# Where a spectral layer asks for its tables and weights: two loads moved from GpSimd's queue to SyncE's, the others asked for earlier, and one table loaded in halves

## The chip, the cores and the metric

The kernel runs on one core of a Trainium2 chip. Its engines are TensorE (PE; its weight loads are listed as PEld), VectorE (DVE), ScalarE (ACT), GpSimd (POOL) and SyncE (SP), each with an instruction stream of its own. They wait for one another by semaphores. Transfers between memory (HBM) and the on-chip memory are asked for by an instruction on SP, ACT or POOL and carried by 16 DMA engines that all queues share; each asking engine has its own queue. The metric is the device time of one execution in microseconds (us), as the median of several runs. A profile is one further execution, recorded instruction by instruction.

## The reference

Two kinds of layer alternate, twice: a spectral layer A and an attention layer B, each on the layer-normed input and added to it.

```python
def _A_ref(x, w_r, w_i):                       # x: [1, 2048, 512]
    X = jnp.fft.rfft2(x.astype(jnp.float32), axes=(-2, -1))
    X = X * (w_r + 1j * w_i)                   # w: [2048, 257]
    return jnp.fft.irfft2(X, s=(S, D), axes=(-2, -1)).astype(jnp.bfloat16)

def _B_ref(x, wq, wk, wv, wo):                 # 32 heads of 16, one shared key and value head
    q = (x @ wq).reshape(B, S, 32, 16).transpose(0, 2, 1, 3)
    k, v = x @ wk, x @ wv
    p = _softmax(jnp.einsum("bhqd,bkd->bhqk", q, k) * 16 ** -0.5, axis=-1)
    o = jnp.einsum("bhqk,bkd->bhqd", p, v)
    return o.transpose(0, 2, 1, 3).reshape(B, S, 512) @ wo

x = A_x
x = x + _A_ref(_layernorm(x), A_w_r, A_w_i)
x = x + _B_ref(_layernorm(x), B_wq, B_wk, B_wv, B_wo)
x = x + _A_ref(_layernorm(x), A_w_r, A_w_i)
x = x + _B_ref(_layernorm(x), B_wq, B_wk, B_wv, B_wo)
```

## The kernel before

The input lies as 16 tiles of 128 rows (`x_sb`, 2 MB in all), in four blocks of four tiles. `full_kernel` asks for the first loads on SP: block 0 of x in two parts, the table `PH` (0.5 MB, the transform along the 512 columns), then blocks 1, 2 and 3 of x with the halves of the tables `S1` and `C1` between them. `feed` takes the layer norm's statistics on DVE, two tiles a step, and makes `S1N`, the negative of `S1`, in two halves.

**The spectral layer** writes the Fourier transforms as matrix products. Its stages, by the names that the profile shows:

- *First loop* (`k` from 0, columns' half `h` = 0): at each step it calls `load(k)` and `feed(k)`, turns two tiles of x (`transpose_pair`, L198 and L201), multiplies them by one half of `PH` (`forward`, L262, result `Pk` on ACT, L184), and rotates them by `C1`, `S1`, `S1N` (`first`, L212 to L214, result `A1`, L274 or L276). Each `A1` goes to memory by a store to `D1` on SP (L277, 128 KB). When the stores that it needs have landed, `cross1` (L280, 256 KB) reads a quarter of `D1` back into `A2` with another part of the rows on the partitions.
- *Second loop* (`h` = 1): `load(10 + k)`, `forward` and `first` with the other half of `PH`, and its own stores and four `cross1`. At k = 7 DVE makes `H2N` from `H2`.
- *Filter loop* (`j` from 0): `filtered(j)` rotates `A2` by the table `G` (L212 to L214, result `X`, L326), and multiplies by the weights `wr_sb` and `wi_sb` on DVE (L330, L332, result `Z`). Steps 0 to 3 read `A2` of the first loop, steps 4 to 7 that of the second. Two steps behind, `back(j)` rotates `Z` by `H1`, `H2N`, `H2` and sends the result `B1` to memory (`D2`, L355).
- Two further stages (`along`, L379, from `B2`, which is read back from `D2`; then `last`) give the columns back and add x.

In the second spectral layer x is turned by DMA transposes during the attention layer before it, save its last tiles, and the last rows of that attention layer's output are made inside the first loop (`rest`).

**What sets the order.** PE, ACT, DVE and SP run in the order in which the code writes their instructions in a spectral layer (`manual_schedule`); POOL isn't in that list, and a scheduler places its instructions. An instruction on SP that waits holds back everything behind it on SP. Eight semaphores go round among the transfers asked for on SP and ACT, so that one also waits for the landing of the one eight before it.

**Where memory is shared.** `wr_sb` lies in the same place as `Kv`, the attention layer's keys (tag `wrkv`). `wi_sb`, `H1` and `H2` lie in a pool of the spectral layer (`tabA`) whose memory the attention layer uses for its own tiles in between. In the second layer their loads wait for the last readers of what lay there. `load` is the function that asks for weights and tables; the weights' runs in memory are 512 bytes long (256 of 257 columns), those of the tables 4096.

Of the kernel before, what the change touches and what calls it, by code (L numbers as in the profile page):

```python
# [11 lines left out]
P = 128  # L12
BF = mybir.dt.bfloat16
# [125 lines left out]
def tile_of(x, k):  # L139
    return x[:, k // 4, k % 4, :]  # L140
# [76 lines left out]
def spectral_layer(nc, tc, tabs, ht, A_w_r, A_w_i, x_sb, bigp, pre, norm, att, feed, weights):  # L217
    C1, S1, S1N, PH, ident = (tabs[n] for n in ("C1", "S1", "S1N", "PH", "ident"))
    with tc.tile_pool(name="workA", bufs=2) as work, tc.tile_pool(name="tabA", bufs=1) as tabA, \
# [7 lines left out]
        wi_sb = tabA.tile([P, 16, 256], BF, name="wi_sb")  # L227
        H1, H2, H2N = (tabA.tile([P, 16, P], BF, name=f"tab_{n}") for n in ("H1", "H2", "H2N"))

        def tables(names):  # L230
            for name in names:
                if tabs[name] is None:
                    tabs[name] = ht.load(tabs["pool"], name)

        def load(k):

            if k == 3:
                nc.sync.dma_start(out=wr_sb, in_=A_w_r.rearrange("(p a) f -> p a f", p=P)[:, :, 1:NF])
            elif k == 6:
                nc.sync.dma_start(out=wi_sb, in_=A_w_i.rearrange("(p a) f -> p a f", p=P)[:, :, 1:NF])  # L240
            elif k == 9:
                tables(("G",))
            elif k == 4:
                ht.load(tabA, "H2", H2, eng=nc.gpsimd)
            elif k == 5:
                ht.load(tabA, "H1", H1, eng=nc.gpsimd)
            elif k == 19:
                tables(("CS", "PSC", "PSS", "hmask"))
            weights(k)
# [35 lines left out]
        for k in range(9 + behind):  # L285
            load(k)
            feed(k, psum)
            if not turned and k < 8:
                transpose_pair(nc, tabs["ident"], psum, x_sb, xT, k, feed.busy or k % 2 == 1, "pa")
            elif turned and LATE_AT <= k < LATE_AT + 2:  # L290
                transpose_pair(nc, tabs["ident"], psum, x_sb, xT, k + 6 - LATE_AT, feed.busy or k % 2 == 1, "pa")
            at = k - behind
            if 0 <= at < 8:
                forward(at, 0)
            if at >= 1:
                first(at - 1, 0)
            if at >= 4 and at % 2 == 0:
                cross1((at - 4) // 2, 0)
        cross1(3, 0)
        for k in range(9):  # L300
            load(10 + k)
            if k < 8:
                forward(k, 1)
            if k >= 1:
                first(k - 1, 1)
            if k >= 4 and k % 2 == 0:
                cross1((k - 4) // 2, 1)
            if k == NEGATE:
                nc.vector.tensor_single_scalar(out=H2N, in_=H2, scalar=-1.0, op=ALU.mult)
        cross1(3, 1)  # L310
        load(19)
        G, CS, PSC, PSS = (tabs[n] for n in ("G", "CS", "PSC", "PSS"))

# [847 lines left out]
@with_exitstack  # L1161
def full_kernel(ctx, tc, A_x, A_w_r, A_w_i, B_x, B_wq, B_wk, B_wv, B_wo, out):
    nc = tc.nc
    const = ctx.enter_context(tc.tile_pool(name="const", bufs=1))
    x_v = A_x.flatten_outer_dims().rearrange("(p r t) d -> p r t d", r=R, t=T)
    x_sb = const.tile([P, R, T, 512], BF, name="x_sb")
    ht = Tables(nc)
    tabs = dict(pool=const, CS=None, PSC=None, PSS=None, hmask=None, G=None)
    tabs["ident"] = ht.load(const, "ident", eng=nc.scalar)
    for part in (slice(0, 2), slice(2, 4)):  # L1170
        nc.sync.dma_start(out=x_sb[:, 0, part, :], in_=x_v[:, 0, part, :])
    tabs["PH"] = ht.load(const, "PH")
    tabs["S1"] = tabs["C1"] = None
    for r in range(1, R):
        nc.sync.dma_start(out=x_sb[:, r, :, :], in_=x_v[:, r, :, :])
        if r < 3:
            for n in ("S1", "C1"):
                tabs[n] = ht.load(const, n, tabs[n], slice(8 * r - 8, 8 * r))
    mhalf = const.tile([P, 4], F32, name="mhalf")
    nc.gpsimd.memset(mhalf, -0.5)  # L1180
    tabs["S1N"] = const.tile([P, 16, P], BF, name="tab_S1N")
    wq_sb = const.tile([P, NC, D], BF, name="wq_sb")
    wk_sb = const.tile([P, NC, DH], BF, name="wk_sb")
    wka = const.tile([P, NC, 8, DH], BF, name="wka")
    wo_sb = const.tile([P, 4, D], BF, name="wo_sb")
    wv_sb = const.tile([P, NC, DH], BF, name="wv_sb")
    xn_sb = const.tile([P, R, T, 512], BF, name="xn_sb")
    lnpool = ctx.enter_context(tc.tile_pool(name="lnpool", bufs=1))
    bigp = ctx.enter_context(tc.tile_pool(name="bigp", bufs=6))
    out_v = out.flatten_outer_dims().rearrange("(p r t) d -> p r t d", r=R, t=T)  # L1190
    att = Attention(nc, tabs, const, bigp, lnpool, wq_sb, wka.rearrange("p c v d -> p c (v d)"), wv_sb, xn_sb)

    def weights(k):
        if k == 19:
            nc.sync.dma_start(out=wk_sb, in_=B_wk.rearrange("(c p) j -> p c j", p=P))
            nc.sync.dma_start(out=wv_sb, in_=B_wv.rearrange("(c p) j -> p c j", p=P))
            for v in range(8):
                nc.gpsimd.tensor_copy(out=wka[:, :, v, :], in_=wk_sb)
        elif k == 20:
            nc.sync.dma_start(out=wq_sb, in_=B_wq.rearrange("(c p) j -> p c j", p=P))  # L1200
            nc.sync.dma_start(out=wo_sb, in_=B_wo.rearrange("(g p) c -> p g c", p=P))

    def make_norm():
        return Norm(nc, lnpool, mhalf, x_sb, xn_sb)

    def store(k, eng=nc.sync):
        eng.dma_start(out=tile_of(out_v, k), in_=tile_of(x_sb, k))

    norm = make_norm()

    def feed(k, psum):

        for t in (0, 1) if k == 0 else ():
            norm.stats(t, tile_of(x_sb, t))
        if k < 7:
            norm.stats(2 * k + 2, tile_of(x_sb, 2 * k + 2))
            norm.stats(2 * k + 3, tile_of(x_sb, 2 * k + 3))
        if k in (2, 5):
            part = slice(0, 8) if k == 2 else slice(8, 16)
            nc.vector.tensor_single_scalar(out=tabs["S1N"][:, part], in_=tabs["S1"][:, part], scalar=-1.0, op=ALU.mult)  # L1220

    feed.busy, feed.xT = True, []
    for layer in range(2):
        norm_in, norm_out = make_norm(), make_norm()
        spectral_layer(nc, tc, tabs, ht, A_w_r, A_w_i, x_sb, bigp, norm, norm_in, att, feed,
                       weights if layer == 0 else lambda k: None)
        feed = attention_layer(nc, tc, att, norm_in, norm_out, x_sb, wo_sb, None if layer == 0 else store)
        norm = norm_out


@with_exitstack
def kernel(
    ctx: ExitStack,
    tc: tile.TileContext,
    A_x: bass.AP,
    A_w_r: bass.AP,
    A_w_i: bass.AP,
    B_x: bass.AP,
    B_wq: bass.AP,
    B_wk: bass.AP,  # L1240
    B_wv: bass.AP,
    B_wo: bass.AP,
    out: bass.AP,
):
    full_kernel(tc, A_x, A_w_r, A_w_i, B_x, B_wq, B_wk, B_wv, B_wo, out)
# [30 lines left out]
```

## Time and profile before

| | |
|---|---|
| runs shown | 1414.59, 1409.14 and 1416.4 us; median 1414.59 |
| the profiled execution | 1412.01 us; its span 1410.2 us |
| mean granted TensorE clock | 0.997 of full |
| PE busy | 1344.2 us (95%), 14050 matmuls |
| ACT busy | 1331.1 us (94%) |
| DVE busy | 1310.5 us (93%) |
| POOL busy | 824.6 us (58%) |
| queue 1 (SP's transfers) | 28.98 MB, 7.2% of 16 engines' span |
| queue 0 (POOL's transfers) | 2.10 MB, 0.4% |
| first spectral layer | from 0 to about 96 us |
| second spectral layer | from about 709 to about 794 us |

The span is the time from the first recorded instruction to the last; the execution's time is a little longer. Busy shares are means over stages with different limits. A row of the timeline gives the start, the duration, the engine, the line of the code, the operation, what is written and read, and in brackets the idle time of the engine before it and what ended that; `SPq` and `POOLq` are issues of a queue. The chain of waits goes back from the last instruction, at each step to what released it.

### The profile page before, as it was taken

The numbers are of one execution on the slowest core, as the hardware profiler recorded it, in microseconds if no ns is written. First come the engines' busy times: TensorE is split into PE (matmuls) and PEld (weight loads), VectorE is DVE, ScalarE is ACT, GpSimd is POOL, SyncE is SP. The second block draws the span as 40 slices with busy tenths as digits, with TensorE's granted clock in tenths as the row PEclk, the third lists the DMA queues.
The fourth block names the chain that finished last, engine by engine and source line by source line (L and its number), as shares of the span: only waits on it lengthen the run. The fifth ranks groups of instructions, "written<-read, shape, count | busy, mean of one in ns | idle before, by whom it ended". The sixth has DMA issues, their size and how long they took to land.

```text
span 1410.2 us, 34818 instructions
## 1 busy us (share of the span) xinstructions
PE 1344.2 (95%) x14050; PEld 471.8 (33%) x14118; DVE 1310.5 (93%) x2271; ACT 1331.1 (94%) x1542; POOL 824.6 (58%) x483
## 2 busy tenths in 40 slices
PE   7799999999999999999997999999999999999998
PEld 6653232223222222222275422332222222222222
DVE  5679999999999999999966899999999999999997
ACT  5679999999999999999955899999999999999997
POOL 2125676667666667667610267666666666666664
PEclk9999999999999999999999999999999999999999
DMA  7700000000000000002064000000000000000000
GB/s 249 210 29 2 1 2 2 2 1 2 2 2 1 2 2 2 1 1 40 8 183 147 2 2 2 2 1 9 5 5 1 6 9 5 2 1 10 9 2 16
DMA packets 44770, 34.52 MB, mean 24 GB/s; under 512 B 10048, under 2 KB 42048, under 8 KB 44096
## 3 DMA queue, kind: packets, MB, share of 16 engines
q1 hardware_dynamic: 41632, 28.98, 7.2%
q8 instruction: 110, 1.80, 0.5%
q0 software_dynamic: 576, 2.10, 0.4%
q10 hardware_dynamic: 2400, 1.21, 0.3%
q14 instruction: 52, 0.43, 0.1%
HBM read 20.22 MB, written 10.49 MB: 22 GB/s over the span
## 4 chain that ended last, share of the span: by engine, by line
ACT 47%; PE 33%; issue 9%; DVE 7%; DMA 3%; POOL 0%; SPq 0%; DVEq 0%; ACTq 0%; POOLq 0%
ACT e L1077 46%; PE pv L866 13%; PE sc L911 11%; DVE ph L951 3%; PE aux L911 2%; PE ps L262 1%; DMA D<-A 1%; PE aux L450 1%; DVE ln_stats L155 1%; DVE ph L983 1%; PE ps L212 1%; DMA x_sb<-in_A_x_dram 1%; DMA B<-D 1%; PE pv L881 1%; PE aux L679 1%
## 5 line engine op out<-in xcount | busy, mean ns | idle before, releaser
L1077 ACT ACTIVATE e<-sc 128x1024 bf16<-128x1024 f32 x1328 | 1218.2, 1166 | 2.9 <-PE sc L911 2.9
L975 POOL TENSOR_TENSOR ph<-ph,step 128x1024 int32<-128x1024 int32 x404 | 762.8, 1891 | 413.1 <-DVE ph L983 293.0
L951 DVE TENSOR_SCALAR ph<-aux 128x512 uint16<-128x512 f32 x1440 | 904.0, 679 | 20.5 <-PE aux L911 15.9
L866 PE MATMUL pv<-ph,vaug 128*32 128x512 bf16 x4320 | 548.8, 386 | 0.7 <-POOL ph L975 0.3
L911 PE MATMUL sc<-QT,Kv 32*128 32x512 bf16 x2656 | 521.8, 380 | 23.5 <-ACT e L1077 16.2
L866 PE MATMUL pv<-e,vaug 128*32 128x512 bf16 x2656 | 483.9, 384 | 0.3 <-ACT e L1077 0.3
L911 PE MATMUL aux<-QT,Kv 32*128 32x512 bf16 x1440 | 455.8, 384 | 1.0 <-DVE ph L951 0.5
L911 PEld LDWEIGHTS <-Kv 32*128 32x128 bf16 x4096 | 183.4, 91 | 525.9 <-issue 517.6
L881 PE MATMUL pv<-wo_sb,zeros 128*32 128x512 bf16 x1200 | 257.8, 383 | 0.0
L866 PEld LDWEIGHTS <-vaug 128*32 128x32 bf16 x6976 | 147.6, 94 | 292.8 <-issue 281.6
L983 DVE TENSOR_SCALAR ph<-ph 128x2048 uint16<-128x2048 uint16 x316 | 216.5, 685 | 0.5
L161 POOL TENSOR_TENSOR ln_rstd<-ln_veps,mhalf 128x4 f32<-128x4 f32 x16 | 16.6, 1036 | 123.7 <-DVE ln_veps L160 123.6
L155 DVE BATCH_NORM_STATS2 ln_stats<-x_sb 128x6 f32<-128x512 bf16 x64 | 43.5, 680 | 28.1 <-ACT x_sb L413 19.4
L881 PEld LDWEIGHTS <-zeros 128*32 128x32 bf16 x1200 | 60.1, 94 | 1.9 <-issue 0.3
L781 DVE STREAM_TRANSPOSE oT<-pv 128x512 f32<-128x512 f32 x64 | 45.2, 707 | 9.2 <-PE pv L866 9.2
L184 ACT ACTIVATE Pk<-ps,ln_rstd 128x256 bf16<-128x256 f32 x64 | 26.8, 474 | 21.9 <-PE ps L262 19.0
L262 PE MATMUL ps<-tab_PH,xT 128*128 128x256 bf16 x256 | 35.3, 286 | 3.9 <-DMA tab_PH<-const_PH 3.0
L276 DVE CAST A<-ps 128x512 bf16<-128x512 f32 x28 | 19.2, 689 | 17.8 <-PE ps L214 17.8
L450 PE MATMUL aux<-xTa,wq_sb 128*128 128x512 bf16 x90 | 32.6, 384 | 2.8 <-issue 2.4
L803 POOL TENSOR_TENSOR on<-oT,rden 128x512 bf16<-128x512 f32 x30 | 31.7, 1056 | 2.0 <-DVE rden L807 1.8
L679 PE MATMUL aux<-wo_sb,ph 128*128 128x512 bf16 x72 | 26.1, 383 | 3.6 <-issue 2.1
L262 PEld LDWEIGHTS <-xT 128*128 128x128 bf16 x256 | 25.1, 102 | 8.1 <-issue 3.7
(109 smaller groups left out, 668.3 us busy)
## 6 DMA issues: line engine op xcount, KB each, us to landing
D<-A SPq DMA_DIRECT2D x32, 128.0 KB, 3.2
A<-D SPq DMA_DIRECT2D x16, 256.0 KB, 3.5
D<-B SPq DMA_DIRECT2D x32, 128.0 KB, 2.5
B<-D SPq DMA_DIRECT2D x12, 256.0 KB, 4.5
tab_H<-const_H POOLq DMA_DIRECT2D x4, 512.0 KB, 6.4
wr_sb<-in_A_w_r_dram SPq DMA_DIRECT2D x2, 1024.0 KB, 6.2
wi_sb<-in_A_w_i_dram SPq DMA_DIRECT2D x2, 1024.0 KB, 7.4
out_dram<-x_sb SPq DMA_DIRECT2D x15, 128.0 KB, 1.7
```

What stands on the lines that cost most here:

```text
L155: nc.vector.bn_stats(st, src)
L262: nc.tensor.matmul(ps[:, j, :], lhsT=xT[:, cc, 2 * k + j, :], rhs=PH[:, cc, 256 * h:256 * h + 256], start=(cc == 0), stop=(cc == NC - 1), ...
L450: self.nc.tensor.matmul(ps, lhsT=w(c), rhs=self.xTq[:, c, qc * 512:(qc + 1) * 512], start=(c == 0), stop=(c == NC - 1), skip_group_check=True)
L679: nc.tensor.matmul(ps, lhsT=OTs[qb][:, g4, kk * P:(kk + 1) * P], rhs=wo_sb[:, g4, :], start=first, stop=last, skip_group_check=True)
L781: end = clock.now(clock.FLIP, lambda: nc.vector.transpose(out=oT[:, par].rearrange("p b c -> p (b c)"), in_=pv), clock.last + clock.MM_END)
L866: nc.tensor.matmul(pv_tiles[gi][32 * i:32 * i + 32, :], lhsT=vaug[:, kc, j, :], rhs=es, start=((gi, i) not in started), stop=(left[gi, i] ...
L881: nc.tensor.matmul(pv_tiles[gi][32 * i:32 * i + 32, :], lhsT=att.zeros, rhs=wo_sb[:, 0, :], start=False, stop=False, skip_group_check=True)
L911: nc.tensor.matmul(out, lhsT=Kv[r, par, kc * P:(kc + 1) * P], rhs=QT[r, g, qb * 512:(qb + 1) * 512], start=True, stop=True, skip_group_che ...
L951: end = clock.now(clock.Z, lambda: nc.vector.tensor_scalar(out=z.bitcast(U16), in0=ps, scalar1=SCALE * LOG2E * 128.0, scalar2=127.0 * 128. ...
L975: nc.gpsimd.tensor_tensor(out=copy.bitcast(I32), in0=z.bitcast(I32), in1=step.to_broadcast([P, w // 2]), op=ALU.add)
L983: nc.vector.tensor_scalar(out=one.bitcast(U16), in0=z.bitcast(U16), scalar1=float(PHASE[1]), scalar2=None, op0=ALU.add)
L1077: nc.scalar.activation(out=e[:, 0:ng * 512], in_=sc[:, 0:ng, :].rearrange("p a b -> p (a b)"), func=ACT.Exp, scale=SCALE)
```

## The change

In `full_kernel`, the table `PH` is asked for in two halves of its columns: the one that the first loop reads stays where the whole was, behind block 0 of x, the other goes behind block 3. In `load`, `H2` and `H1` are asked for on SP and not on POOL. In the first spectral layer (`first_layer`) `wr` stays at step 3, `wi` goes from step 6 to 4, `H2` from 4 to 6 and `H1` from 5 to 8. In the second all four are asked for at step 0, ahead of all stores to `D1`. `G` and the later tables stay where they were. No engine but SP and POOL has an instruction added, removed or moved.

```diff
+        first_layer = tabs["G"] is None
+
         def load(k):
 
-            if k == 3:
+            at = (3, 4, 6, 8) if first_layer else (0, 0, 0, 0)
+            if k == at[0]:
                 nc.sync.dma_start(out=wr_sb, in_=A_w_r.rearrange("(p a) f -> p a f", p=P)[:, :, 1:NF])
-            elif k == 6:
+            if k == at[1]:
                 nc.sync.dma_start(out=wi_sb, in_=A_w_i.rearrange("(p a) f -> p a f", p=P)[:, :, 1:NF])
-            elif k == 9:
+            if k == at[2]:
+                ht.load(tabA, "H2", H2)
+            if k == at[3]:
+                ht.load(tabA, "H1", H1)
+            if k == 9:
                 tables(("G",))
-            elif k == 4:
-                ht.load(tabA, "H2", H2, eng=nc.gpsimd)
-            elif k == 5:
-                ht.load(tabA, "H1", H1, eng=nc.gpsimd)
             elif k == 19:
                 tables(("CS", "PSC", "PSS", "hmask"))
             weights(k)
...
-    tabs["PH"] = ht.load(const, "PH")
+    tabs["PH"] = const.tile([P, 4, 512], BF, name="tab_PH")
+    ph = nc.inline_tensor(ht.host["PH"], name="const_PH").ap()
+    nc.sync.dma_start(out=tabs["PH"][:, :, 0:256], in_=ph[:, :, 0:256])
     tabs["S1"] = tabs["C1"] = None
     for r in range(1, R):
         nc.sync.dma_start(out=x_sb[:, r, :, :], in_=x_v[:, r, :, :])
         if r < 3:
             for n in ("S1", "C1"):
                 tabs[n] = ht.load(const, n, tabs[n], slice(8 * r - 8, 8 * r))
+    nc.sync.dma_start(out=tabs["PH"][:, :, 256:512], in_=ph[:, :, 256:512])
```

## The prediction

> **What bounds the kernel now.** I read the page first, then the chain of waits in order of time, then the timeline and SP's queue in the two spectral layers, and last the windows there.
>
> ```profile
> span 1410.2 us, 34818 instructions
> ...
> DMA  7700000000000000002064000000000000000000
> ...
> ACT 47%; PE 33%; issue 9%; DVE 7%; DMA 3%; POOL 0%; SPq 0%; DVEq 0%; ACTq 0%; POOLq 0%
> ```
>
> The attention layers, bound by ACT and PE, make most of the span. Transfers fill the DMA engines in slices 0, 1 and 18 to 21 only: the spectral layers, and only these can the change shorten. The order of instructions on PE, DVE and ACT is the same before and after; SP's order changes, and POOL loses its four table loads. So the question is which waits on transfers end sooner or later.
>
> The start, in the timeline (start, duration, engine, in brackets the idle time before and who ended it):
>
> ```profile
> 2.31 0.76 POOL L135 DMA_DIRECT2D tab_H<-const_H  x1
> 3.21 0.54 POOL L135 DMA_DIRECT2D tab_H<-const_H  x1
> ...
> 8.91 1.86 PE L262 MATMUL ps<-tab_PH,xT 128*128 128x256 bf16 x8 [3.00 <-DMA tab_PH<-const_PH]
> ...
> 11.97 0.69 DVE L155 BATCH_NORM_STATS2 ln_stats<-x_sb 128x6 f32<-128x512 bf16 x1 [4.47 <-DMA x_sb<-in_A_x_dram]
> ...
> 15.38 0.42 DVE L1220 TENSOR_SCALAR tab_S1N<-tab_S 128x1024 bf16<-128x1024 bf16 x1
> ...
> 15.86 0.29 PE L214 MATMUL ps<-Pk,tab_S1N 128*128 128x128 bf16 x1 [0.80 <-DVE tab_S1N L1220]
> ```
>
> The code asks for H2 and H1 at steps 4 and 5, but POOL's order isn't written by hand, so they start at 2.31 and 3.21, amid the loads of x, PH, S1 and C1. The second block of x ends the long wait: DVE sits idle 4.47 us until it lands, and its statistics lead to S1N, for which PE waits.
>
> **The start, step by step.** The time from issue to landing of these two table loads (minimum, median, maximum), and two windows of layer 1 (the last number is GB/s):
>
> ```profile
> DMA to landing us min/median/max: 8.6/9.1/9.6
> ```
> ```profile
> 12.00:14.00 2.00, 2.00 (x14) 1.69 (x15) 1.93 (x5) 0.93 (x1) 0.00 (x0) 1.00 1.06 414
> ...
> 22.00:24.00 2.00, 2.00 (x27) 1.87 (x25) 1.93 (x6) 2.00 (x5) 0.00 (x0) 1.00 1.10 288
> 24.00:26.00 2.00, 2.00 (x26) 1.86 (x25) 1.82 (x6) 2.00 (x5) 0.00 (x0) 1.00 0.28 75
> ...
> 34.00:36.00 2.00, 2.00 (x24) 1.84 (x23) 0.80 (x2) 1.38 (x4) 0.00 (x0) 1.00 0.61 168
> ```
>
> Long runs go at 414 GB/s, runs of 512 bytes (wr, wi, D1) at 288. H2 and H1 are 1.05 MB: 2.53 us of the DMA engines' time. By 11.95, when x lands, the first of them has landed (2.31 + 8.6) and the second not (3.21 + 9.6), so between 1.27 and 2.53 us stood before x; I take 1.9. PH was 0.52 MB at 414, 1.27 us; its half has runs of 512 bytes, 0.26 MB at 288, 0.91 us: 0.36 less. So x lands 2.3 us sooner, and DVE, S1N and PE's first rotation move with it. PH's first half lands sooner as well, and the 1.86 us of matmuls that it gates still end before S1N; the other half comes last of the start's loads and is wanted only by the second loop. A further 0.3 us may come because PE has no pause between its first groups: the engines are 2.6 us earlier, between 1.9 and 2.9. The additional issue on SP costs nothing, as what SP issues next, the first store to D1, comes only after PE's rotation at 15.86. POOL is spared 1.3 us of issuing, and its next instruction waits for DVE.
>
> **The queue in layer 1.** SP's own timeline there, PE's wait, and the landing time of wr:
>
> ```profile
> 17.75 0.66 SPq L238 DMA_DIRECT2D wr_sb<-in_A_w_r_dram  x1
> 20.57 4.13 SPq L277 DMA_DIRECT2D D<-A  x3
> 25.52 0.34 SPq L280 DMA_DIRECT2D A<-D  x1
> 25.92 0.55 SPq L240 DMA_DIRECT2D wi_sb<-in_A_w_i_dram  x1
> ...
> 33.42 2.23 SPq L280 DMA_DIRECT2D A<-D  x2
> ...
> 42.81 3.06 SPq L280 DMA_DIRECT2D A<-D  x2
> ```
> ```profile
> 48.98 0.27 PE L212 MATMUL ps<-A,tab_G 128*128 128x256 bf16 x1 [1.17 <-DMA tab_CS<-const_CS]
> ```
> ```profile
> DMA to landing us min/median/max: 6.1/6.1/6.1
> ```
>
> PE's filter loop needs A2, which needs the stores to D1 before it. Of the first loop's four A2 loads the last is issued at 33.42 + 2.23 - 0.32 = 35.33 us, when the last D1 has landed (0.32 is a typical issue). SP issues in order, so the second loop's stores stand behind it, and so on to the last A2 load at 42.81 + 3.06 - 0.32 = 45.55 and to PE's wait at 48.98 (put down to tab_CS, which lands at about that time; what PE's instruction reads is A2). So what counts for layer 1 is when that D1 lands.
>
> From wr's issue the queue carries wr and wi (1.05 MB each), seven D1 (0.92), two A2 (0.52) and G (0.1): 3.64 MB, 12.6 us at 288. It took 17.6, since wi is only asked for at 25.92, behind stores and an A2 that wait; the queue had run dry (75 GB/s). Now wi follows the second D1, at 20.57 - 2.6, before wr is through. H2 and H1 add 2.53: 15.2 us without a gap. Of wr's 6.1 us to landing 3.6 are data, so 2.5 are lead. From 17.75 - 2.6 = 15.15 that ends at 32.9: 2.4 sooner. A2's reads run slower than 288 (168 in 34 to 36), so I take 2.0; the bounds are 0 (a mean of 220 GB/s instead of 288) and 2.9 (the engines). PE reaches the filter loop's second half 2.6 us sooner and waits 0.6 us more than the 1.17 it had. **Layer 1: 2.0.**
>
> **Layer 2.** Timeline, and one row of the chain in order of time:
>
> ```profile
> 706.20 0.39 PE L911 MATMUL sc<-QT,Kv 32*128 32x512 bf16 x2
> ...
> 708.95 1.19 POOL L135 DMA_DIRECT2D tab_H<-const_H  x2 [2.14 <-PE pv L866]
> ...
> 723.55 2.89 SPq L277 DMA_DIRECT2D D<-A  x1
> ...
> 724.85 0.69 DVE L276 CAST A<-ps 128x512 bf16<-128x512 f32 x1 [0.18 <-PE ps L214]
> ...
> 736.13 0.68 DVE L276 CAST A<-ps 128x512 bf16<-128x512 f32 x1
> 736.26 0.27 PE L212 MATMUL ps<-A,tab_G 128*128 128x256 bf16 x1 [0.51 <-DVE tab_H2N L309]
> ...
> 740.48 2.54 SPq L280 DMA_DIRECT2D A<-D  x2
> ...
> 746.53 0.37 PE L212 MATMUL ps<-A,tab_G 128*128 128x256 bf16 x1 [2.96 <-DMA A<-D]
> ...
> 746.91 0.42 PE L212 MATMUL ps<-A,tab_G 128*128 128x256 bf16 x1
> ```
> ```profile
> 727.49 5.34 DMA D<-A
> ```
>
> The last D1 of the first loop has its data at 724.85 + 0.69 = 725.54, but SP issues it at 727.49 (an earlier store stood 2.89 us behind wi) and it takes 5.34 us, to 732.83. Only then can its A2 go, then the second loop's stores, then its last A2 at 740.48 + 2.54 - 0.32 = 742.70, and PE waits 2.96 us, until 746.53.
>
> After the change wr waits on SP for Kv's last reader (706.20 + 0.39) and the other three for PE to let go of the tables' memory, for which POOL waited until 708.95. Queued behind them on SP are the stores to D1. 2.1 MB at 288 and 1.05 at 414 are 9.8 us: done about 719. The first stores land later than now, and nobody waits for them, since PE reads A2 only after the second loop. From then on the queue is empty when a store comes: the last D1 goes out at 725.6 and lands near 728. The second loop's stores go as their data are made, the last at 736.13 + 0.68 = 736.81. It shares the queue with A2 loads, so I put the last A2 issue at 739.5; with the 3.8 us that it now takes from there to PE, that is 743.3. Without its two waits PE would be there at 746.53 - 2.96 - 0.51 = 743.06. So PE starts 3.2 us sooner (2 if a wait of 1.3 is left), and no longer at half rate behind the pause (0.42 us for a matmul of 0.27). What the rate is worth I bound by layer 1, where the same work ran at full rate:
>
> ```profile
> 69.01 1.05 PE L379 MATMUL ps<-tab_CS,B 128*128 128x256 bf16 x8 [2.09 <-DMA B<-D]
> ```
> ```profile
> 768.37 0.83 PE L379 MATMUL ps<-tab_CS,B 128*128 128x256 bf16 x6 [1.71 <-DMA B<-D]
> ```
>
> From the filter loop's second half to these matmuls it is 20.03 us there and 21.84 here, 1.8 apart. ACT and DVE had rested in the pause, which they no longer do; I take 1.2, bounds 0 and 1.8. **Layer 2: 4.4**, bounds 2 and 5.
>
> **The sum:** 2.0 + 4.4 = 6.4 us. The profiled execution took 1412.01 us (span 1410.2), 2.6 below the median of the runs shown, 1414.59 (1409.14 to 1416.4). Taken off these, 1405.6 and 1408.2; between them I say 1406.5, and price the rivals from 1412.9. The bound of 0.5%, about what a measurement of this kernel can tell from no change, is 7 us.
>
> **The rivals.** The landing times of wi and of the tables in layer 2:
>
> ```profile
> DMA to landing us min/median/max: 8.1/8.1/8.1
> ```
> ```profile
> DMA to landing us min/median/max: 3.6/3.9/4.3
> ```
>
> - *The tables eat layer 1's gain.* On POOL's queue they shared the DMA engines with the stores; on SP's they and wi stand whole before the last D1, and at a mean of 220 GB/s it lands when it does now. For it: 168 in 34 to 36; against: 288 while wr moves. Gain 4.4: 1408.5. Chance 0.15. (The Trainium skill, DMA: Bandwidth & Descriptors, Queues, rings and completion order, says that a DMA engine takes packets from its queue rows in turn but consumes one row in ring order. By that rule this is what moving the tables to SP costs; the store that stood 2.89 us behind wi agrees.)
> - *Half rate in layer 1.* PE's new pause there, 1.8 us, lets its rate drop as that of 2.96 did; 1.8 us lost, gain 4.6: 1408.3. Against: the pauses of 2.09 and 1.71 above, with full rate behind them. Chance 0.1. (The Trainium skill, TensorE: Matmul & The Clock Gate, Part 1, asks for an idle window of about 3.4 us; the trace drops after 2.96 already.)
> - *Queue no limit.* Layer 1 gets the engines' 2.9 and layer 2 all 5.0: 7.9, 1405.0. For it: in layer 2 the queue is empty from 719. Chance 0.28.
> - *Slower: loads in series hold the stores.* If the four loads each took their present time to land one after the other, layer 1 would bear 6.1 twice, 4.3 twice, seven D1 of 0.46 and two A2 of 0.91 from 15.15, and issue that A2 near 41 instead of 35.33; in layer 2 6.1, 8.1 and twice 4.3 from 707 end near 730, eight D1 near 734, A2 near 738, when PE has wanted it since 736. Some 7.5 us more: 1420. It decides if the loads don't overlap at all. Against: 414 and 288 GB/s while several are in flight. Chance 0.07.
> - *Not at once.* A reader of the tables' memory later than 708.95 holds wi and the tables, and layer 2 gains nothing: 2.0, 1410.9. Chance 0.05.
>
> **How the numbers follow.** Forecast 0.35, rivals as given. Faster by over 0.5%: 0.21 of "no limit", 0.16 of the forecast (its upper part), and 0.05 of the two cases near 4.5, by the runs' own spread: 0.42. Slower by over 0.5%: the series case, and 0.01 for that spread: 0.08. The rest, 0.50, lies within 0.5%. The range leaves out the series case and the ends of the runs' spread (7 us over three): 1400.5 to 1413.
>
> **What would show it.** Right: x's second block ends DVE's wait near 9.6 us; the fourth A2 load of layer 1 is issued near 33; PE waits under 0.5 us for A2 in layer 2, with matmuls of 0.27 behind it. Wrong: that A2 issued later than 35.3, a wait of PE in layer 1 over 3 us, or a wait left in layer 2.

## The result, and the profile after

The changed kernel takes 1406.64 us (median of 12 runs, 1402.94 to 1409.38), the kernel before, in runs beside it, 1413.22 (12 runs): a ratio of 0.9957 [0.9942, 0.9971], so by the ratio 6.1 us less (4.1 to 8.2). The forecast was 1406.5. The profiled execution took 1406.44 us, where the one before took 1412.01: 5.6 less. Of the span, 1.85 us are gone before layer 2's first matmul (709.23 before, 707.38 after) and 3.7 behind it.

The page after, its span and its DMA share in 40 slices, which differs from the one before by a digit in slices 0, 2, 18 and 20, in the spectral layers:

```profile
span 1404.7 us, 34813 instructions
...
DMA  8710000000000000001074000000000000000000
```

The start, in the timeline of the kernel after:

```profile
5.94 1.89 PE L265 MATMUL ps<-tab_PH,xT 128*128 128x256 bf16 x8 [0.25 <-ACT xT L201]
...
8.67 1.03 PE L198 MATMUL pst<-tab_ident,x_sb 128*128 128x128 bf16 x8 [0.84 <-DMA x_sb<-in_A_x_dram]
...
12.53 0.23 PE L214 MATMUL ps<-Pk,tab_S1N 128*128 128x128 bf16 x1 [0.81 <-DVE tab_S1N L1226]
```

In this execution PE no longer waits for PH. x's second block ends PE's wait at 8.67 and DVE's just before, instead of 11.97, and the first rotation with `S1N` comes at 12.53 instead of 15.86: the engines are 3.3 us earlier.

Layer 1's queue (SP's timeline), and of PE's timeline the two waits for `A2` in the filter loop and the first matmul of `along` on the second half of the columns, called *tab_CS* from here on:

```profile
16.84 0.56 SPq L243 DMA_DIRECT2D wi_sb<-in_A_w_i_dram  x1
...
29.63 4.80 SPq L283 DMA_DIRECT2D A<-D  x2
34.48 2.05 SPq L280 DMA_DIRECT2D D<-A  x4
...
41.72 2.69 SPq L283 DMA_DIRECT2D A<-D  x2
```
```profile
37.65 0.27 PE L212 MATMUL ps<-A,tab_G 128*128 128x256 bf16 x1 [1.56 <-DMA D<-A]
...
48.04 0.28 PE L212 MATMUL ps<-A,tab_G 128*128 128x256 bf16 x1 [3.10 <-DMA A<-D]
...
69.04 1.05 PE L382 MATMUL ps<-tab_CS,B 128*128 128x256 bf16 x8 [1.90 <-DMA B<-D]
```

The fourth A2 load goes out at 29.63 + 4.80 - 0.32 = 34.11 (35.33 before), the last at 44.09 (45.55). So of the engines' 3.3 us 1.2 are left at the one and 1.5 at the other; PE makes up the difference in waits of 1.56 and 3.10 us (before, none and 1.17), and at tab_CS nothing is left in these two executions: 69.04, where it was 69.01.

Layer 2, SP's timeline and PE's:

```profile
704.77 0.57 SPq L241 DMA_DIRECT2D wr_sb<-in_A_w_r_dram  x1
706.64 0.59 SPq L243 DMA_DIRECT2D wi_sb<-in_A_w_i_dram  x1
707.28 3.81 SPq L135 DMA_DIRECT2D tab_H<-const_H  x2
...
735.46 1.77 SPq L283 DMA_DIRECT2D A<-D  x2
```
```profile
707.38 0.38 PE L265 MATMUL ps<-tab_PH,xT 128*128 128x256 bf16 x2 [0.81 <-DVE oT L784]
...
740.88 0.27 PE L212 MATMUL ps<-A,tab_G 128*128 128x256 bf16 x1
...
763.00 1.05 PE L382 MATMUL ps<-tab_CS,B 128*128 128x256 bf16 x8 [1.70 <-DMA B<-D]
```

The row at 740.88 has no wait in brackets, and the matmul takes 0.27 us, full rate (0.42 at half rate). From layer 2's first matmul to it, it is 33.50 us; before it was 746.53 - 709.23 = 37.30. From there to tab_CS it is 22.12, where it was 21.84.

### The profile page after: what moved, and what is told of

Same layout as the page of the kernel before. It is cut to its first block, busy times and chain, and to the rows that moved or that the text cites. A ratio compares the mean times of both kernels' runs of the same rounds, so it can differ in the third digit from the quotient of the medians.

```text
span 1404.7 us, 34813 instructions
## 1 busy us (share of the span) xinstructions
PE 1341.2 (95%) x14050; PEld 470.1 (33%) x14118; DVE 1309.9 (93%) x2271; ACT 1330.7 (95%) x1542; POOL 821.4 (58%) x479
## 4 chain that ended last, share of the span: by engine, by line
ACT 50%; PE 32%; issue 9%; DVE 6%; DMA 2%; POOL 0%; SPq 0%; DVEq 0%; ACTq 0%
ACT e L1080 49%; PE pv L869 12%; PE sc L914 10%; DVE ph L954 2%; PE aux L914 2%; PE ps L265 1%; DVE ln_stats L155 1%; PE ps L212 1%; PE aux L453 1%; DMA B<-D 1%; DMA D<-B 1%; PE pv L884 1%; DVE ph L986 1%; PE aux L682 1%; DMA x_sb<-in_A_x_dram 0%
## 5 line engine op out<-in xcount | busy, mean ns | idle before, releaser
L954 DVE TENSOR_SCALAR ph<-aux 128x512 uint16<-128x512 f32 x1440 | 903.8, 678 | 20.4 <-PE aux L914 15.9
L385 ACT CAST AT<-ps 128x512 bf16<-128x512 f32 x24 | 14.1, 595 | 14.1 <-PE ps L382 14.1
```

Of the source, the lines that this page charges most:

```text
L954: end = clock.now(clock.Z, lambda: nc.vector.tensor_scalar(out=z.bitcast(U16), in0=ps, scalar1=SCALE * LOG2E * 128.0, scalar2=127.0 * 128. ...
```

## The experiments

**Layer 2's half of the change alone.** PH is whole and layer 1's loads are as before (the code is shown against the changed kernel, lines between left out as ...):

```diff
-            at = (3, 4, 6, 8) if first_layer else (0, 0, 0, 0)
+            at = (3, 6, 4, 5) if first_layer else (0, 0, 0, 0)
...
-                ht.load(tabA, "H2", H2)
+                ht.load(tabA, "H2", H2, eng=nc.gpsimd if first_layer else None)
...
-                ht.load(tabA, "H1", H1)
+                ht.load(tabA, "H1", H1, eng=nc.gpsimd if first_layer else None)
```

> Only the second layer is changed: there H2, H1 and both weights are asked for at step 0 on SP; the first layer and PH are as before. Theory (the forecast's layer 2): the first layer's rows stay (fourth A2 load issued near 35.3 us, PE's 1.17 us wait near 49), in the second the last store to D1 of the first loop lands within 3 us of its issue, PE has no wait over 0.5 us for A2, and from its first PH matmul to the first G matmul of the filter loop's second half it takes 33.5 us instead of 37.3; time 3.5 us lower, ratio 0.9975. Rival (the second layer gains only because the first one ends elsewhere, or because POOL's loads are gone from the start): a wait of PE over 2 us is left, ratio within 0.0008 of 1.

1408.14 us (12 runs), ratio 0.9969 [0.9956, 0.9981]: 4.4 us less, between 2.7 and 6.2. The first and the last row of the stretch, 742.32 - 708.82 = 33.50 us, no wait for A2, full rate:

```profile
708.82 0.60 PE L265 MATMUL ps<-tab_PH,xT 128*128 128x256 bf16 x4 [0.81 <-DVE oT L784]
...
742.32 0.27 PE L212 MATMUL ps<-A,tab_G 128*128 128x256 bf16 x1
```

**Layer 1's half alone** (PH in halves, layer 1 as changed; layer 2 as before):

```diff
-            at = (3, 4, 6, 8) if first_layer else (0, 0, 0, 0)
+            at = (3, 4, 6, 8) if first_layer else (3, 6, 4, 5)
...
-                ht.load(tabA, "H2", H2)
+                ht.load(tabA, "H2", H2, eng=None if first_layer else nc.gpsimd)
...
-                ht.load(tabA, "H1", H1)
+                ht.load(tabA, "H1", H1, eng=None if first_layer else nc.gpsimd)
```

> Only the first layer is changed (PH in halves, wi at step 4, H2 and H1 on SP at 6 and 8); the second is as before, its tables on POOL. Theory A (the forecast's layer 1): 2.0 us lower, ratio 0.9986, through a fourth A2 load issued 1 to 2 us sooner than 35.3, and the second layer keeps its 3 us wait. Theory B (what the changed kernel's trace suggests): the engines are 3.3 us sooner in the first loop, but the queue gives back all: PE's pause before the filter loop's second half is 3 us, TensorE drops to half rate behind it, and the rows of B2 (near 69 us) start where they did before; what is won, 0 to 1.7 us, depends on where half rate falls in the stage behind. Ratio 0.9988 to 1.0.

1410.6 us, ratio 0.9991 [0.998, 1.0001]: 1.3 us less, not told from none. In its trace layer 1 has a pause of PE as the changed kernel has, with tab_CS at 68.92, and layer 2 has its wait and half rate back:

```profile
47.95 0.28 PE L212 MATMUL ps<-A,tab_G 128*128 128x256 bf16 x1 [2.43 <-DMA A<-D]
...
745.94 0.37 PE L212 MATMUL ps<-A,tab_G 128*128 128x256 bf16 x1 [2.99 <-DMA D<-B]
```

**PH in halves, nothing else** (the kernel before with the change's edits in `full_kernel` alone):

> The kernel before with only PH in halves; the tables stay on POOL at the start. Theory: the second block of x lands 0.4 to 0.8 us sooner than 11.95, the first PH matmul 1 us or more sooner than 8.91, and by the fourth A2 load (35.3) no more than 0.5 us of it is left: ratio 0.9997. Rival (it was PH and not the tables that held x): x lands near 9, as in the changed kernel, ratio 0.998.

1409.71 us, ratio 0.9992 [0.998, 1.0004]: not told from none, and not told from layer 1's whole half (0.9991) either.

```profile
8.77 0.37 PE L262 MATMUL ps<-tab_PH,xT 128*128 128x256 bf16 x1 [3.04 <-DMA tab_PH<-const_PH]
...
11.13 0.69 DVE L155 BATCH_NORM_STATS2 ln_stats<-x_sb 128x6 f32<-128x512 bf16 x1 [3.82 <-DMA x_sb<-in_A_x_dram]
```

PE still waits 3.04 us for half of PH, with POOL's two table loads beside it, and x comes 0.84 us sooner than 11.97; in the changed kernel, without them, it came 3.3 sooner. It was mostly those two loads, and not PH's size, that held the start.

**Layer 1 at once too**, as layer 2:

```diff
-            at = (3, 4, 6, 8) if first_layer else (0, 0, 0, 0)
+            at = (0, 0, 0, 0)
```

> The changed kernel, with the first layer also asking for all four at step 0. Theory (the queue of layer 1 is bound by running dry and by tables late in it): the loads fill the queue right behind the start's, from 14 to 24 us; the stores that wait behind them are not late for anyone, and the fourth A2 load is issued near 31 us instead of 34.1, PE's pause before the filter loop's second half is under 1.5 us, no half rate behind it: 1.5 to 3 us below the changed kernel, ratio to the kernel before 0.9940. Rival (what stands ahead of a store costs it as much): the fourth A2 load is issued at 34 or later, ratio 0.9955 or above.

1406.38 us, ratio 0.9954 [0.994, 0.9969]: not told from the changed kernel's 0.9957. SP's timeline:

```profile
9.64 5.28 SPq L243 DMA_DIRECT2D wi_sb<-in_A_w_i_dram  x1
...
29.15 0.44 SPq L280 DMA_DIRECT2D D<-A  x1
30.06 4.00 SPq L283 DMA_DIRECT2D A<-D  x2
```

The last of the four loads landed at 25.4, yet the fourth A2 load went out at 30.06 + 4.00 - 0.32 = 33.74, hardly sooner than 34.11, and PE paused 2.97 us at 47.69. So in layer 1 it is not the loads' bytes alone that set this load: the store that it needs had its data at 27.24, was issued only at 29.15, behind an A2 load that had waited on SP, and landed near 33.7.

**The tables later in layer 1**, behind the first loop's stores and A2 loads:

```diff
-            at = (3, 4, 6, 8) if first_layer else (0, 0, 0, 0)
+            at = (3, 4, 10, 11) if first_layer else (0, 0, 0, 0)
```

> The changed kernel, with layer 1's H2 and H1 asked for at steps 10 and 11, behind the first loop's stores and A2 loads. Theory (the 1.05 MB of the tables stand before the stores that the fourth A2 load waits for): that load goes out near 32 instead of 34.11, 2.5 us of transfer less ahead of it, PE's wait at the first half (1.56 us) is gone; the second half's A2 comes no sooner, since the tables then stand before the second loop's stores; time within 1 us of the changed kernel's. Rival (not the bytes but the landing of stores one behind the other sets it): the fourth A2 load within 0.7 us of 34.11.

1410.59 us, ratio 0.999 [0.9979, 1.0002]. The theory has the fourth A2 load about right and the time wrong: by the ratios 4.7 us of the gain are lost, and the intervals are apart.

```profile
29.17 4.01 SPq L283 DMA_DIRECT2D A<-D  x2
33.24 0.89 SPq L135 DMA_DIRECT2D tab_H<-const_H  x2
...
41.15 0.32 SPq L283 DMA_DIRECT2D A<-D  x1
```
```profile
51.67 0.39 PE L212 MATMUL ps<-A,tab_G 128*128 128x256 bf16 x1 [7.55 <-DMA tab_CS<-const_CS]
```

The fourth A2 load goes out at 32.86, 1.25 sooner than in the changed kernel, and sooner than in all five other traces with that layer 1 up to there (33.94 to 35.62): that much or more the tables cost it. But the second loop's stores, now behind the tables, land so late that its first A2 load waits until 41.15 (37.92 in the changed kernel), and PE 7.55 us. In this layer a table asked for later on SP stands before stores that somebody waits for.

**The A2 loads of layer 1 on POOL's queue:**

```diff
-            nc.sync.dma_start(out=A2[32 * g:32 * g + 32, h, :, :],
+            eng = nc.gpsimd if first_layer else nc.sync
+            eng.dma_start(out=A2[32 * g:32 * g + 32, h, :, :],
```

> The changed kernel, but layer 1's eight A2 loads are asked for on POOL's queue, so that no store to D1 stands behind an A2 load that waits on SP. Theory (SP's order gives the engines' lead back): the first loop's last store is issued within 1 us of its data instead of 28.83, the fourth A2 load goes out by 32 instead of 34.11, the last one by 42 instead of 44.09, PE's pause at the filter loop's second half falls from 3.10 us to under 1.5, and the execution is some 1.5 to 2.5 us shorter, near 1404.5. Rival (the transfers' own bytes bound it): the last A2 load is issued within 0.7 us of 44.09, the pause stays over 2.3 us and the time is within 0.7 us of the changed kernel's.

1408.35 us, ratio 0.9974 [0.9962, 0.9987], by the ratios 2.4 us worse than the changed kernel, with intervals that just overlap; tab_CS comes at 70.78. The reason is one that neither theory had:

```profile
23.20 0.74 POOL L284 DMA_DIRECT2D A<-D  x1 [4.53 <-DMA D<-A]
23.97 1.03 POOL L161 TENSOR_TENSOR ln_rstd<-ln_veps,mhalf 128x4 f32<-128x4 f32 x1
```

The A2 load waited 4.53 us on POOL, and behind it stood the layer norm's ln_rstd, for which ACT and through it PE waited (1.89 us at 25.56). The wait was only moved to another engine that works in order. It doesn't tell the theories apart.

**The fourth A2 load behind the second loop's first four stores**, still on SP, layer 1 only:

```diff
-        cross1(3, 0)
+        if not first_layer:
+            cross1(3, 0)
...
+            if k == 4 and first_layer:
+                cross1(3, 0)
             if k >= 4 and k % 2 == 0:
```

> The changed kernel, but in layer 1 SP issues the first loop's fourth A2 load after the second loop's first four stores to D1 and not ahead of them. Theory (the stores of the second loop, whose data are there from 28.05 us on, stand on SP behind that A2 load, which waits until 34.11 for its last store): these four stores go out between 29 and 32.5 instead of 34.48 to 36.04, the fourth A2 load still near 34, the last A2 load near 41 instead of 44.09, PE's pause of 3.10 us at the filter loop's second half falls under 1 us, and the execution is 1 to 3 us shorter than the changed kernel's, about 1404.5. Rival (the DMA engines' throughput sets when A2 lands, in whatever order it is asked for): the last A2 load lands within 1 us of 48.00, the pause stays above 2 us, no gain. Second rival (it lands sooner but the transfers of the back-transform take the gain, as they took that of the full rate): the pause is gone, but the second half's first matmul on tab_CS stays within 0.5 us of 69.04.

1402.78 us (6 runs), ratio 0.9937 [0.992, 0.9954]: the fastest of all. Its SP timeline and PE's:

```profile
30.48 2.81 SPq L280 DMA_DIRECT2D D<-A  x4
34.54 1.60 SPq L283 DMA_DIRECT2D A<-D  x2
...
39.68 2.80 SPq L283 DMA_DIRECT2D A<-D  x2
```
```profile
46.78 0.28 PE L212 MATMUL ps<-A,tab_G 128*128 128x256 bf16 x1 [1.79 <-DMA A<-D]
...
66.41 0.28 PE L385 MATMUL ps<-tab_CS,B 128*128 128x256 bf16 x1 [1.59 <-DMA B<-D]
```

Four stores go out from 30.48 on instead of 34.48, the fourth A2 load loses only 0.4 us (34.54), the last one goes out at 42.16 instead of 44.09, the pause is 1.79 instead of 3.10, and tab_CS is reached at 66.41, 2.6 us before 69.04 (in the three profiles with the changed layer 1 as it is, it is 68.34 to 69.04). That is the theory's direction at each of its points, though not its size at the pause (under 1 us was expected). By the ratios it is 2.8 us under the changed kernel (0.9937 against 0.9957), with intervals that overlap, so the size of the gain rests on the trace.

**Ten unread matmuls in PE's pause** of layer 1, to keep its rate:

```diff
+            if first_layer and j == 4:
+                ps = psum.tile([P, 512], F32, name="ps", tag="pa")
+                for _ in range(10):
+                    nc.tensor.matmul(ps, lhsT=ident, rhs=PH[:, 0, :], start=True, stop=True,
+                                     skip_group_check=True)
             if j < 8:
                 filtered(j)
```

> The changed kernel with ten additional matmuls of 128x512 on PE (never read) ahead of the filter loop's second half in layer 1, where PE pauses 3.10 us; they fit into the pause. Theory (half rate behind the pause costs what the granted clock says: 0.64 for 4 us and 0.93 for 4 more): full rate behind it, the second half's back-transform (first matmul on tab_CS of the second half) starts 1.7 us sooner than 69.04, and the execution is some 1.5 us shorter. Rival (ACT and DVE, which copy and multiply behind PE, set that stretch whatever PE's rate): full rate, but that matmul within 0.4 us of 69.04 and no gain.

1405.73 us (6 runs), ratio 0.9951 [0.9934, 0.9968], not told from the changed kernel's. Windows of the changed kernel, then of this one (the third number from the end is the granted clock, then DMA share and GB/s), and its row of tab_CS:

```profile
48.00:52.00 4.00, 3.96 (x35) 3.47 (x36) 2.08 (x4) 2.65 (x5) 1.81 (x5) 0.64 0.88 258
52.00:56.00 4.00, 3.84 (x49) 3.45 (x48) 2.89 (x6) 3.73 (x8) 0.73 (x5) 0.93 0.30 101
```
```profile
48.00:52.00 4.00, 3.23 (x42) 2.90 (x43) 1.86 (x4) 2.96 (x6) 0.99 (x3) 1.00 0.97 286
52.00:56.00 4.00, 3.72 (x49) 3.21 (x48) 3.87 (x9) 3.82 (x9) 2.48 (x6) 1.00 0.39 128
...
69.06 0.28 PE L386 MATMUL ps<-tab_CS,B 128*128 128x256 bf16 x1 [1.77 <-DMA B<-D]
```

The clock is full again, and tab_CS comes at 69.06 all the same. The lost rate (0.36 and 0.07 of 4 us each: 1.7 us) costs nothing there. What PE waits for at 69.06 is B2, and not ACT or DVE, as the rival had it. On SP the second half's B2 loads stand behind the first half's four and the six D2 stores that follow those.

**Blocks 2 and 3 back-transformed ahead of the filter of block 4**, to fill the pause with work:

```diff
+            if j == 4:
+                joined()
+                back(2)
+                back(3)
             if j < 8:
                 filtered(j)
...
-            if j >= 2:
+            if j in (2, 3) or j >= 6:
                 back(j - 2)
```

> The changed kernel, with the back-transforms of blocks 2 and 3 put ahead of the filter of block 4 on PE, ACT and DVE (both layers), so that PE has 1.7 us of work of its own in the pause of layer 1. Theory: the pause falls from 3.10 us to about 1.4, the rate stays full, two blocks fewer are left behind it, and the second half's first matmul on tab_CS comes 1.5 to 2.5 us sooner than 69.04; in layer 2, which has no pause there, within 0.5 us; the execution about 2 us shorter, 1404.5. Rival (the DVE and ACT work ahead of these blocks makes PE wait just as long, now for Z): that matmul within 0.5 us of 69.04, layer 2 up to 1 us longer, no gain or a loss of 1 us.

1408.4 us (7 runs), ratio 0.9967 [0.9954, 0.9979]: no gain, and by the ratios a loss of 1.4 us as the rival had it, with intervals that overlap. In layer 2:

```profile
765.28 0.40 PE L386 MATMUL ps<-tab_CS,B 128*128 128x256 bf16 x1 [2.98 <-DMA B<-D]
```

In layer 1 PE waits for Z instead (1.36 and 0.34 us) and reaches the filter of block 4 at 49.96, not 48.04, and tab_CS at 69.22, and in layer 2 the filter of block 4 comes behind two blocks that it didn't wait for: from the layer's first matmul to tab_CS it is 57.7 us there, 55.6 in the changed kernel.

**Layer 2's tables on POOL again, its weights early on SP:**

```diff
-            at = (3, 4, 6, 8) if first_layer else (0, 0, 0, 0)
+            at = (3, 4, 6, 8) if first_layer else (0, 0, 4, 5)
...
-                ht.load(tabA, "H2", H2)
+                ht.load(tabA, "H2", H2, eng=None if first_layer else nc.gpsimd)
...
-                ht.load(tabA, "H1", H1)
+                ht.load(tabA, "H1", H1, eng=None if first_layer else nc.gpsimd)
```

> The changed kernel, with layer 2's H2 and H1 asked for on POOL at steps 4 and 5 as before the change; wr and wi stay at step 0 on SP. Theory (what counts in layer 2 is that wi stands ahead of the stores to D1): from layer 2's first forward matmul to the filter loop's second half 33.5 us, within 0.7, and no wait of PE for A2, like the changed kernel. Rival (the tables' move to SP is what counts): 35 us or more, and a wait of PE for A2 over 1 us is back; time near 1409.

1406.17 us (5 runs), ratio 0.9956 [0.994, 0.9973].

```profile
706.69 0.38 PE L265 MATMUL ps<-tab_PH,xT 128*128 128x256 bf16 x2 [0.81 <-DVE oT L784]
...
740.19 0.27 PE L212 MATMUL ps<-A,tab_G 128*128 128x256 bf16 x1
```

33.50 us, as in the changed kernel. In layer 2 the whole gain comes from asking for wr and wi first; which queue the tables are on makes no difference that shows.

**The second half's D2 stores on ACT's queue**, both layers, so that they don't stand behind the B2 loads on SP:

```diff
-                nc.sync.dma_start(out=D2[h, :, b:b + 2, :], in_=B1[:, h, b:b + 2, :])
+                eng = nc.scalar if j >= 4 and not (j == 7 and b > b4) else nc.sync
+                eng.dma_start(out=D2[h, :, b:b + 2, :], in_=B1[:, h, b:b + 2, :])
```

> The changed kernel, with the second half's stores to D2 (all but the last, whose data come from DVE) issued on ACT's queue instead of SP's, in both layers, so that they do not stand in a ring behind the four B2 loads of the first half. Theory (they wait in SP's ring): they land within 3 us of their issue instead of 4 to 7, the last of them 1.5 to 3 us sooner after the first B2 load's issue (8.7 us in layer 1, 10.7 in layer 2), and the execution is 2 to 4 us shorter, about 1403.5. Rival (the DMA engines are full in that stretch, 304 GB/s, and B2's and D2's bytes take as long in any order): that interval within 0.7 us of 8.7 and 10.7, B2 lands later by as much as D2 lands sooner, time within 1 us of the changed kernel's or up to 1 us longer for ACT's issuing.

1404.68 us (6 runs), ratio 0.9951 [0.9934, 0.9968]: not told from the changed kernel's. From the issue of the first B2 load to the landing of the last D2 store it is 10.1 us in layer 1 and 9.7 in layer 2, against 8.7 and 10.7. The transfers of this stretch take some 9 to 11 us on either queue. From the filter loop's second half to tab_CS it is 20.4 and 20.8 us in this trace, against 21.0 and 22.1.

**The two together:**

> The two edits that gained, together: layer 1's fourth A2 load behind the second loop's first four stores, and the second half's D2 stores on ACT's queue in both layers. If their gains add (3 us and some 1 us in the traces against the changed kernel): the pause at layer 1's second half under 2 us, the stretch from there to the second half's first matmul on tab_CS 19.6 to 20.6 us, and in layer 2 20.8; about 1402. If ACT's issuing takes back what the other queue gives: 1403 to 1404, no better than the first edit alone at 1402.8.

1403.48 us (6 runs), ratio 0.9947 [0.9926, 0.9967]; 20.48 us from the filter loop's second half to tab_CS in layer 1, 20.77 in layer 2. The stretches are as short as expected, the time is that of the second case: nothing over the later A2 load alone.

Its trace is a second one with the later A2 load. From the first rotation with `S1N` to the issue of layer 1's last A2 load it is 29.9 us there and 29.1 with the later load alone. In the six traces with these stores and loads in the changed kernel's order it is 30.9 to 32.1, and in the three with layer 1's tables at the start, as before, 29.7 to 30.3. So in layer 1 the change lengthens this stretch, and one A2 load put behind four stores undoes that: the order on SP is what gave the lead back.

## Why the forecast held, and which of its steps did not

**The sum and its layer 2 term.** 6.4 us were forecast and 6.1 measured. In layer 2 it was to be 4.4, and layer 2's half alone gives 4.4 (2.7 to 6.2); in the profiled execution it is 3.7. The route was the one forecast. The last D1 of the first loop, its issue and its time to landing:

```profile
723.72 0.36 SPq L280 DMA_DIRECT2D D<-A  x1
```
```profile
DMA to landing us min/median/max: 2.5/2.5/2.5
```

So it landed near 726.2, that is 728.1 with the 1.85 us by which layer 2 starts sooner here; 728 was forecast. The last A2 load goes out at 735.46 + 1.77 - 0.32 = 736.91, 738.8 on that clock (739.5 forecast), and PE reaches the second half 33.5 us into the layer (34.1 forecast). It waits for no A2 there; of the seven other traces with this layer 2 one, that of the ten unread matmuls, has a wait of 0.88 us.

**Within it one part was mis-sized: the full rate.** 1.2 us were to come because PE no longer runs at half rate behind its pause. The stretch from the second half to tab_CS was to be 20.6 us and is 22.12, longer than before, so in this pair of traces nothing of it came. But this trace has the longest of eight: the seven others with the same layer 2 have 19.9 to 21.9, and all eight 21.3 on average. With layer 2 as before, the two traces at half rate have 21.84 and 22.66, and that of PH in halves, where the rate stayed full behind a wait of 3.19 us, has 21.25. So the rate is worth some 0.6 to 1.0 us, an estimate from these averages, and the pauses gave 3.8 us (3.2 forecast). That the sum came out to the digit is luck, as one part was larger than forecast and the other smaller.

What PE waits for at tab_CS is B2, 1.70 us after and 1.71 before. The time from issue to landing (minimum, median, maximum) of the four B2 loads of layer 2, before, after, and of the six D2 stores behind them, after:

```profile
DMA to landing us min/median/max: 2.9/5.0/6.0
```
```profile
DMA to landing us min/median/max: 2.9/5.7/7.2
```
```profile
DMA to landing us min/median/max: 5.4/6.3/7.0
```

**Layer 1's term had its route wrong.** The forecast counted the bytes ahead of the first loop's last D1 and let it land when they end. That step failed. The last `A1` of the first loop and its store, before and after:

```profile
29.76 0.58 ACT L274 CAST A<-ps 128x512 bf16<-128x512 f32 x1 [0.47 <-PE ps L214]
30.72 0.49 SPq L277 DMA_DIRECT2D D<-A  x1
```
```profile
25.17 0.59 ACT L277 CAST A<-ps 128x512 bf16<-128x512 f32 x1 [0.47 <-PE ps L214]
28.83 0.44 SPq L280 DMA_DIRECT2D D<-A  x1
```

The data are there 4.6 us sooner, at 25.76, but the store goes out only 1.9 sooner: it stands 3.1 us on SP (0.4 before), behind an A2 load that goes out at 26.96, and it lands after 5.2 us (4.5 before). So the fourth A2 load, which was to go out 2.0 us sooner, went 1.22. Taking that load's issue as the whole of layer 1's gain was the second fault. From it to the landing of the last A2 it is 13.4 us before and 13.9 after, because the second loop's stores stand behind it on SP. The forecast saw that, but not that the data of those stores are ready while it waits, from 28.05 on, so that the place of this one instruction counts too. With it moved, tab_CS comes at 66.41, and at 67.78 in the kernel with both edits; the change alone brought nothing there that shows.

PE's pause, 1.8 forecast, became 3.10, which is over the 3 us that the forecast had named as a sign of being wrong. In three other traces with this layer 1 up to there it is 1.95, 2.33 and 2.43.

Two readings in this term don't hold. By its own terms the gain is nought at a mean of 240 GB/s; at the 220 that it names, the load would go out 1.4 us later than before. And 168 GB/s in the window 34 to 36 was read as the speed of A2's reads, but its row has the DMA engines busy 0.61 of the time.

The start was forecast well. In this pair of traces x comes 3.3 us sooner (2.3 forecast), but the pair lies at the ends of a spread: x's second block ends DVE's wait at 11.97 and 11.51 in the two traces with PH whole and the tables on POOL, at 11.13 with PH in halves alone, and at 8.65 to 9.65, with a median of 9.15, in the eleven with the changed start. By these, PH's half gives some 0.4 to 0.8 (0.36 forecast) and the tables about 2.0 (1.9 forecast).

What layer 1's half is worth over many runs is 1.3 us (-0.1 to 2.8) alone and 1.7 beside layer 2's (0.9957 against 0.9969): not told from none, nor from the 2.0 forecast. Where it sits is not settled. In the two profiled executions all of it lies behind tab_CS, and there it is chance: the execution before dropped to half rate in the last transform (windows of before; after, the clock is 1.00 in both):

```profile
68.00:72.00 4.00, 2.75 (x14) 1.52 (x15) 0.36 (x1) 1.78 (x4) 0.00 (x0) 0.84 1.15 327
72.00:76.00 4.00, 4.00 (x19) 1.98 (x17) 2.97 (x8) 2.83 (x6) 0.00 (x0) 0.74 0.39 124
```

That is 0.16 and 0.26 of 4 us, 1.7 in all. With layer 1 exactly as before, in the profile of layer 2's half alone, tab_CS comes at 70.32 and not 69.01, and no such drop follows. So two executions of one arrangement differ there by as much as this half of the change is worth.

**The rivals.** *The tables eat layer 1's gain* came true in part: moved behind, they let the fourth A2 load out 1.25 us sooner, so they had cost it that. But with them it still went out 1.22 sooner than before, and on SP they are no worse than further back, since the stores that would go behind them cost more than 4 us. (The Trainium skill, DMA: Bandwidth & Descriptors, Queues, rings and completion order, has a DMA engine take packets from its queue rows in turn. By that, tables on POOL's row should hold SP's stores less. The runs don't test it: in layer 2 it is 33.50 us with the tables on either row, and PE waited for no A2 in either. The 2.89 us by which the forecast had the trace agree are the time that SP took to issue that store, so they show the order on SP rather than that in the row.) *Half rate in layer 1* came true in place, and its price of 1.8 us did not: the rate fell to 0.64, and with it full again tab_CS came no sooner. The forecast's evidence against it was misread: full rate was seen just behind the wait of 2.09 at 69.01, and by the window from 72 on the rate was at 0.74. *Queue no limit* is refuted for layer 1 by the waits of 1.56 and 3.10. *Loads in series* did not happen: the tables of layer 2, the last of its four loads, landed by 718.5. *Not at once* did not happen either: wi went out at 706.64 and the tables at 707.28.

## What to carry to other kernels

Where one queue carries stores and loads in order, look for a load that waits while stores with finished data stand behind it, before looking at how many bytes are ahead: moving that one load behind four stores brought the next stage 2.6 us forward in the trace, where the whole change had brought nothing; by the medians it gave 2.8 us, with intervals that overlap. A wait moved to another in-order engine takes that engine's own work with it. And before a difference of 1 or 2 us between two traces is explained, look at other traces with the same stretch: x's landing, the pause in layer 1 and the way to tab_CS differ by 1 to 2 us between executions of the same code. Price a stretch by what is late at its end: in layer 1 PE's half rate was seen, measured and cured, and no gain showed, as the next wait was for a transfer.

## What the hardware showed that was not expected

PE's rate drops behind waits shorter than supposed, and not always. Behind the pause in layer 1 it dropped after 2.43 and 2.97 us (layer 1's half alone, layer 1 at once) and after 1.95 (layer 2's tables on POOL: 0.53 in the window 48 to 50), and stayed full after 1.79 and 1.34. With PH in halves alone it stayed full behind 2.70 us in layer 1 and 3.19 in layer 2. With D2 on ACT's queue a wait of 2.33 was followed by full rate, and one of 1.98, which ended at 58.07, by a drop (windows of that kernel):

```profile
58.00:60.00 2.00, 1.59 (x16) 1.32 (x17) 1.37 (x4) 0.97 (x3) 0.00 (x0) 0.84 0.98 262
60.00:62.00 2.00, 2.00 (x15) 1.56 (x14) 0.61 (x1) 0.88 (x2) 0.00 (x0) 0.50 0.99 324
```

The Trainium skill, TensorE: Matmul & The Clock Gate, Part 1, has windows of about 3.4 us that run freely, so that the moment of a change depends on where in one the work falls. That the same length of wait goes both ways agrees with it; that waits of 1.95 and 1.98 are enough does not, where it asks for a whole idle window.

SP's issue of a load can itself take long: 5.28 us for wi asked for right behind wr, 3.81 for the two tables of layer 2. In layer 2 nothing that stood behind it came too late: PE waited for no A2.
